# Values in two groups a visit, and one landing place for queries and keys, in a threshold attention with token and channel MLPs

## The chip, the cores and the metric

One NeuronCore of one Trainium2 chip runs the whole program. The metric is the device time of one execution in microseconds, here the median of the runs shown. Everything is float32 on the engines; TensorE runs each float32 matmul as two instructions.

The engines are named as in the profile: PE is TensorE's matrix multiply and PEld its loading of weights, DVE is VectorE, ACT is ScalarE, POOL is GpSimd, and SP is SyncE, which computes nothing here and issues transfers. SPq and ACTq are the queues on which SP and ACT issue transfers.

## The reference

Inputs are q, k and v of shape (8 batches, 8 heads, 576 tokens, 64), a threshold `tau` of 0.02, and four weight matrices, which arrive as 64-bit floats.

```
scores = (q @ k^T) / 8
keep the scores within tau of their row's maximum, set the rest to -1e9
attn = softmax(scores);  x = attn @ v, heads laid side by side: (8, 576, 512)
u = x + (relu(x^T @ w_tok1) @ w_tok2)^T        # over tokens, 576 -> 256 -> 576
out = u + relu(u @ w_ch1) @ w_ch2              # over channels, 512 -> 1536 -> 512
```

## The kernel before

Heads are worked in pairs, four pairs to a batch, 32 pairs in all. Two pairs (a half batch) are cut into 9 units: units 0 to 3 are the 128-row blocks of the first pair, unit 4 is shared and holds the last 64 rows of both pairs, and units 5 to 8 are the 128-row blocks of the second pair. The program has 144 units, 18 to a batch, in one hand-written loop over `u` (L534 to L587); every engine takes its instructions in the order in which that loop writes them, and so do the transfer queues.

For each unit the loop writes, in this order:

- `scores(u)` (L287): 8 TensorE instructions (16 in the shared unit) into the PSUM tiles `sc`, one for each head; DVE takes the row maxima (L306), POOL turns them into biases (L307).
- `norm(u-1)` (L327): DVE's reciprocal of the row sums, POOL's scaling of the previous unit's exponentials `e` (L334).
- The transposition of unit u-2. In batch 0 TensorE does it through PSUM (`turn`, L345). From batch 1 on (`in_blocks`) DVE transposes 32x32 blocks into a tile `T` (L368) and SP's queue moves the blocks into place with 16 transfers (L378) into a tile `eT`, once a group is complete. A group is two units of one pair (rows 0 to 255, or 256 to 511), or the shared unit alone.
- A share of the MLP steps that the previous batch left (`fill`), then `weigh(u)` (L310): ACT's two Prelus (L316), a share of `fill`, two exponentials (L323) with a share of `fill` behind each. A batch's MLP steps are queued by `push` when its last values group is written, and `fill` spreads them by their estimated costs over the next batch's units.
- The loads of queries and keys of a later pair (`load_qk`, L97), in quarters of 32 partitions, q and k each: 8 transfers of 72 KB for a pair; in batch 0 SP issues them, later ACT. `load_v` issues one transfer of a pair's values.
- `prep` (L278): DVE transposes a pair's loaded queries and keys into `qT` and `kT` (L283), which have two places each. It is written in units 2 and 7 of a half batch.
- The values groups that are due (`values`, L390): 20 TensorE instructions, L408 and L413, in pairs that use half of the array's columns each, into a PSUM tile `pv` (`pv_s` for the shared rows), and ACT's copy of it into `xT` (L418). PSUM has two tiles (`ps_tr`) for this, shared with the transposes.

In batch 0 the loop also converts the weights from 64 bits to float32 in 31 pieces (`weight`, `load_piece`): SP loads a piece (L176) into one of four raw places, ACT takes two steps (L191, L193), DVE three (L201, L205, L209), POOL one (L215). The conversion goes on in batch 1, whose units also carry batch 0's MLP. ACT, DVE, POOL and SP meet these steps in the same queues as the units' own work.

A group's values are written two units after its transposition (one in batch 0). Within the 9 units of a half batch, counted from its first, the groups from batch 1 on come at the end of unit 5 (first pair, rows 0 to 255), 7 (first pair, rows 256 to 511), 8 (shared, two small groups), 1 of the next half (second pair, first rows) and 3 of the next half (second pair, last rows).

Of the kernel before, what the change touches and what calls it, by code (L numbers as in the profile page):

```python
# [9 lines left out]
F32 = mybir.dt.float32  # L10
# [7 lines left out]
P = 128  # L18
# [3 lines left out]
def kernel(  # L22
# [26 lines left out]
    nc = tc.nc  # L49
    B, H, S, D = q.shape  # L50
# [14 lines left out]
    NK = 2 * S // P  # L65
# [4 lines left out]
    ld = ctx.enter_context(tc.tile_pool(name="ld", bufs=2))  # L70
    work = ctx.enter_context(tc.tile_pool(name="work", bufs=2))
# [11 lines left out]
    pairs = [(b, p) for b in range(B) for p in range(NP)]  # L83
# [9 lines left out]
    loaded = {}  # L93
    VL = 4
    vlast = [const.tile([P, P], F32, name=f"vl{i}") for i in range(VL)]

    def load_qk(n, eng, part=None):  # L97


        b, p = pairs[n]  # L100
        if n not in loaded:
            loaded[n] = [ld.tile([P, S // 32, 32], F32, tag=tag, name=f"{tag}_{n}") for tag in ("lq", "lk")]
        for i in range(4) if part is None else (part,):
            h, c = divmod(i, 2)
            for src, t, on in zip((q, k), loaded[n], eng):
                on.dma_start(
                    out=t[32 * i : 32 * i + 32], in_=src[b, 2 * p + h, :, 32 * c : 32 * c + 32].rearrange("(n t) d -> t n d", t=32)
                )

    def load_v(n):  # L110

        b, p = pairs[n]
        lv = ld.tile([P, NK, D], F32, tag="lv", bufs=4, name=f"lv_{n}")
        nc.sync.dma_start(out=lv, in_=v[b].rearrange("h s d -> (h s) d")[2 * S * p : 2 * S * p + 2 * S, :].rearrange("(c p) d -> p c d", p=P))
        vals[n] = lv
# [51 lines left out]
    def load_piece(i):  # L167
        if i >= len(pieces):
            return
        dst, src = pieces[i]  # L170
        rows = dst.shape[0]
        n = 1
        for d in dst.shape[1:]:
            n *= d
        raw = raw_at[i % NRAW][0:rows, 0 : n * (2 if wide(i) else 1)].bitcast(src.dtype)
        nc.sync.dma_start(out=like(raw, dst), in_=src)  # L176
        if wide(i):
            words = raw.bitcast(U32).rearrange("p (n w) -> p n w", w=2)
            h2 = work.tile([P, WMAX], F32, tag="o", name=f"h2_{i}")[0:rows, 0:n]
            raws[i] = like(words[:, :, 0], dst), like(words[:, :, 1], dst), like(h2, dst)  # L180
        else:
            raws[i] = like(raw, dst)
# [40 lines left out]
    def weight(n):  # L223

        nonlocal steps_done
        for k in range(steps_done, min(steps_done + n, 3 * len(pieces) + 1)):
            i, part = divmod(k, 3)
            if part == 0:
                on_gpsimd(i - 1)
                if i:  # L230
                    load_piece(i - 1 + NRAW)
            else:
                on_scalar(i + 1, part - 1)
            on_vector(i, part)
            steps_done = k + 1
# [3 lines left out]
        weight(3 * i + 4 - steps_done)  # L239

    load_piece(0)
    load_qk(1, (nc.sync, nc.sync))
    load_v(0)
    for i in range(1, NRAW):
        load_piece(i)
# [26 lines left out]
    eTs = {}  # L272
    Ts = {}

    def in_blocks(b):
        return b > 0

    def prep(n):  # L278
        lq, lk = loaded.pop(n)
        made = []  # L280
        for src, name in ((lq, "qT"), (lk, "kT")):
            sb = work.tile([P, S], F32, tag=name, name=f"{name}_{n}")
            nc.vector.transpose(out=sb, in_=src.rearrange("p n d -> p (n d)"))  # L283
            made.append(sb)
        heads[n] = made
# [41 lines left out]
    def norm(u):  # L327
        e, rs = st[u]
        rr = small.tile([P, 2], F32, tag="rr", name=f"rr_{u}")
        nc.vector.tensor_scalar(out=rr, in0=rs, scalar1=1e-9, scalar2=None, op0=ALU.add)  # L330
        nc.vector.reciprocal(out=rr, in_=rr)  # L331
        for h in range(2):
            eh = e[:, S * h : S * h + S]
            nc.gpsimd.tensor_scalar(out=eh, in0=eh, scalar1=rr[:, h : h + 1], scalar2=1.0, op0=ALU.mult, op1=ALU.mult)  # L334
        st[u] = e

    def group_of(u):

        b, p0, t = units[u]
        if t == SHARED:  # L340
            return (b, p0, "s"), 0, 1
        i, c = divmod(t - (t > SHARED), NI)
        return (b, p0 + i, c // 2), c % 2, 2

    def turn(u, third):  # L345

        key, place, n = group_of(u)
        e = st[u]
        if third == 0 and place == 0:
            eTs[key] = work.tile([P, NK * 2 * P], F32, tag="eT", name=f"eT_{u}")  # L350
        if third == 2:
            st.pop(u)
        eT = eTs[key][:, 0 : NK * n * P].rearrange("p (c x) -> p c x", c=NK)
        ps = ps_tr.tile([P, MAIN], F32, tag="tr", name=f"tr{third}_{u}")[:, 0 : 3 * P].rearrange("p (c x) -> p c x", c=3)
        for c in range(3):
            k0 = (3 * third + c) * P
            nc.tensor.transpose(out=ps[:, c, :], in_=e[:, k0 : k0 + P], identity=ident)
        on = nc.scalar.copy if third == 1 and u % 2 else nc.vector.tensor_copy
        on(out=eT[:, 3 * third : 3 * third + 3, P * place : P * place + P], in_=ps)

    def turn_blocks(u):

        key, place, n = group_of(u)
        e = st.pop(u)
        if place == 0:
            Ts[key] = work.tile([P, NK * 2 * P], F32, tag="T", name=f"T_{u}")
        T = Ts[key][:, 0 : NK * n * P]
        nc.vector.transpose(  # L368
            out=T.rearrange("p (a c n x) -> p c a n x", a=4, c=NK, n=n)[:, :, :, place, :],
            in_=e.rearrange("p (c a x) -> p c a x", c=NK, a=4),  # L370
        )
        if place == n - 1:
            del Ts[key]
            eTs[key] = work.tile([P, NK * 2 * P], F32, tag="eT", name=f"eT_{u}")
            w = NK * n * 32
            for a in range(4):
                for i in range(4):
                    nc.sync.dma_start(  # L378
                        out=eTs[key][32 * a : 32 * a + 32, w * i : w * i + w], in_=T[32 * i : 32 * i + 32, w * a : w * a + w]
                    )  # L380

    def split_middle(n):

        lv, vl = vals[n], vlast[n % VL]
        for h in range(2):
            r = slice(D * h, D * h + D)
            nc.gpsimd.tensor_copy(out=vl[r, r], in_=lv[r, NI, :])
        vals[n] = lv, vl
# [140 lines left out]

    prep(0)  # L530
    due = deque()
    b_now = 0
    LAG = 2
    for u in range(len(units) + LAG + 4):  # L534
        on = u < len(units)
        if u == UB:
            late.close()
            ps_mm = ctx.enter_context(tc.tile_pool(name="ps_mm", bufs=2, space=bass.MemoryType.PSUM))
        if on:
            b_now, p0, t = units[u]  # L540
            n = b_now * NP + p0
        w = u - LAG
        back = 0 <= w < len(units)
        if on:
            scores(u)
        if 0 < u <= len(units):
            norm(u - 1)
        if b_now:
            weight(2)
        if back:  # L550
            key, place, many = group_of(w)
            if in_blocks(key[0]):
                turn_blocks(w)
            else:
                for i in range(3):
                    turn(w, i)
            if place == many - 1:
                b, p, c = key
                if c == 0 and p % 2 == 0:
                    split_middle(b * NP + p)  # L560
                if c == "s":
                    split_middle(b * NP + p + 1)
                when = u + (2 if in_blocks(b) else 1)
                due += [(when, b, p + i, c) for i in range(2 if c == "s" else 1)]
        if b_now:
            fill(0.4)
        weight(2 if b_now else 1)
        if on:
            weigh(u)
        elif b_now:  # L570
            fill(0.6)
        weight(2 if b_now else 1)
        if on:
            m = n + 2 + t // 4
            if t < 8 and m < len(pairs):
                load_qk(m, (nc.scalar if b_now else nc.sync,) * 2, t % 4)
                if t % 4 == 3:
                    load_v(m)
            if t == 2:
                prep(n + 1)  # L580
            if t == 7 and n + 2 < len(pairs):
                prep(n + 2)
        while due and due[0][0] <= u:
            _, b, p, c = due.popleft()
            values(b, p, c)
            if p == NP - 1 and c == 1:
                push(b)  # L587
# [31 lines left out]
```

## Time and profile before

| | |
|---|---|
| median of 3 runs | 1392.27 us (1392.06 to 1392.32) |
| profiled execution | 1392.27 us, span 1390.5 us |
| TensorE, matmuls | 1325.5 us busy, 95% of the span |
| DVE | 586.8 us, 42% |
| ACT | 590.0 us, 42% |
| POOL | 357.8 us, 26% |
| granted TensorE clock, mean | 0.991 |
| matmuls: channel MLP, first (L468) / second (L484) | 398.6 / 389.1 us |
| matmuls: scores (L301) | 190.1 us |
| matmuls: values, 128x256 groups (L408 / L413) | 42.4 / 123.5 us |

The span runs from the first to the last instruction. The 40 slices of a page are 34.8 us each; a digit is the busy share in tenths. Rows of a timeline give the start, the length, the engine, the line, the operation with output and inputs, and how many instructions of that kind follow each other; the bracket at the end is the engine's idle time ahead of the row and what ended it. A row of the chain of waits gives a start, a length and what the time went to. TensorE's instructions are pipelined, so rows that follow each other overlap a little; starts are what to subtract.

### The profile page before, as it was taken

What the parts mean: (1) busy time and instruction counts of PE and PEld (TensorE: products, weight loads), DVE (VectorE), ACT (ScalarE), POOL (GpSimd) and SP (SyncE); (2) the same over time, 40 slices, a digit from 0 to 9 for tenths busy, and PEclk for the clock granted to TensorE, in tenths of its full rate; (3) what the DMA queues carried; (4) which work ended last, traced back from release to release, by engine and by line L of the source; (5) the groups of instructions that cost most, each with busy time, mean ns of one, the idle gap of its engine ahead of it and who ended that gap; (6) DMA issues with size and microseconds to landing.
All of it is one profiled execution on the core that took longest, in us unless ns stands there. A gap on an engine that the chain in (4) does not pass through costs nothing.

```text
span 1390.5 us, 19515 instructions
## 1 busy us (share of the span) xinstructions
PE 1325.5 (95%) x6866; PEld 831.8 (60%) x6866; DVE 586.8 (42%) x1009; ACT 590.0 (42%) x1328; POOL 357.8 (26%) x683
## 2 busy tenths in 40 slices
PE   6776899999999999999999999999999999999998
PEld 3443475646565566665766567465657566575675
DVE  6788784444444444434244344433343453101000
ACT  5776564444454444443434435353434444120110
POOL 4566563232222222212122222221221222000000
PEclk9998899999999999999999999999999999999999
DMA  6444654444444434433433444443433433300000
GB/s 132 97 115 125 185 140 122 109 120 93 107 118 107 105 86 97 109 84 79 110 85 92 104 96 102 98 105 79 99 91 89 103 76 85 84 8 16 8 8 23
DMA packets 257376, 128.34 MB, mean 92 GB/s; under 512 B 208064, under 2 KB 221376, under 8 KB 257280
## 3 DMA queue, kind: packets, MB, share of 16 engines
q1 hardware_dynamic: 131632, 111.46, 30.5%
q10 hardware_dynamic: 125648, 15.64, 7.1%
q8 instruction: 55, 0.90, 0.3%
q14 instruction: 41, 0.34, 0.1%
HBM read 43.25 MB, written 9.44 MB: 38 GB/s over the span
## 4 chain that ended last, share of the span: by engine, by line
PE 86%; DVE 6%; DMA 2%; ACT 2%; SPq 2%; POOL 1%; issue 1%; DVEq 0%; ACTq 0%
PE c L484 27%; PE c L468 26%; PE sc L301 11%; PE pv L413 7%; PE t L439 5%; PE t L446 3%; PE pv L408 2%; DVE mx L306 2%; PE tx L430 1%; SPq L378 1%; PE c L480 1%; PE pv_s L413 1%; DVE T L368 1%; DMA scratch<-in_moe_w_ch_dram 1%; ACT e L316 1%
## 5 line engine op out<-in xcount | busy, mean ns | idle before, releaser
L306 DVE TENSOR_REDUCE mx<-sc 128x1 f32<-128x576 f32 x288 | 204.7, 751 | 523.1 <-PE sc L301 521.1
L468 PE MATMUL c<-xT,wc 128*128 128x256 f32 (+1 forms) x1920 | 398.6, 361 | 0.5 <-ACT g L469 0.4
L484 PE MATMUL c<-wc,g 128*128 128x512 f32 x864 | 389.1, 596 | 0.0
L468 PEld LDWEIGHTS c<-xT,wc 128*128 128x128 f32 x1920 | 334.3, 190 | 69.7 <-issue 27.6
L307 POOL TENSOR_SCALAR bias<-mx,toff 128x1 f32<-128x1 f32 x288 | 79.6, 277 | 814.9 <-DVE mx L306 757.9
L316 ACT ACTIVATE e<-sc,bias 128x576 f32<-128x576 f32 x288 | 199.2, 739 | 155.5 <-POOL bias L307 155.1
L484 PEld LDWEIGHTS c<-wc,g 128*128 128x128 f32 x864 | 157.9, 190 | 175.3 <-issue 173.2
L469 ACT ACTIVATE g<-c 128x256 f32<-128x256 f32 (+1 forms) x240 | 86.7, 361 | 335.5 <-PE c L468 330.6
L334 POOL TENSOR_SCALAR e<-e,rr 128x576 f32<-128x576 f32 x288 | 218.8, 772 | 16.0 <-DVE rr L331 3.8
L323 ACT ACTIVATE e<-e,ntau 128x576 f32<-128x576 f32 x288 | 220.6, 771 | 0.0
L301 PE MATMUL sc<-kT,qT 64*128 64x288 f32 (+1 forms) x1280 | 190.1, 435 | 14.2 <-DVE kT L283 7.2
L368 DVE STREAM_TRANSPOSE T<-e 128x1152 f32<-128x1152 f32 x126 | 172.5, 1369 | 16.3 <-DMA eT<-T 9.6
L301 PEld LDWEIGHTS sc<-kT,qT 64*128 64x128 f32 (+1 forms) x1280 | 103.7, 179 | 90.0 <-issue 47.6
L413 PE MATMUL pv<-eT,lv 128*64 128x256 f32 x1024 | 123.5, 384 | 0.0
L413 PEld LDWEIGHTS pv<-eT,lv 128*64 128x64 f32 x1024 | 75.1, 139 | 37.5 <-issue 0.8
L489 DVE COPY o<-c 128x512 f32<-128x512 f32 x36 | 24.5, 679 | 160.8 <-PE c L484 160.8
L446 PE MATMUL t<-w,a 128*128 128x288 f32 x256 | 79.0, 438 | 13.6 <-DVE xT L450 10.4
L418 ACT COPY xT<-pv 128x256 f32<-128x256 f32 x64 | 23.8, 372 | 160.0 <-PE pv L413 147.2
L439 PE MATMUL t<-x_sb,w 128*128 128x512 f32 x160 | 73.2, 605 | 0.7 <-ACT g L469 0.7
L446 PEld LDWEIGHTS t<-w,a 128*128 128x128 f32 x256 | 46.8, 198 | 41.4 <-DVE xT L450 18.4
L450 DVE TENSOR_TENSOR xT<-xT,t 128x288 f32<-128x288 f32 x64 | 28.0, 441 | 81.9 <-PE t L446 81.9
L323 ACT ACTIVATION_READ_ACCUMULATOR e<-e,ntau 128x1 f32 x288 | 56.5, 196 | 0.0
(48 smaller groups left out, 603.2 us busy)
## 6 DMA issues: line engine op xcount, KB each, us to landing
eT<-T SPq DMA_DIRECT2D x896, 72.0 KB, 2.1
scratch<-in_moe_w_ch_dram SPq DMA_DIRECT2D x24, 512.0 KB, 4.0
lv<-in_v_dram SPq DMA_DIRECT2D x32, 288.0 KB, 3.3
out_dram<-o SPq DMA_DIRECT2D x36, 256.0 KB, 2.2
eT<-T SPq DMA_DIRECT2D x224, 36.0 KB, 1.9
lk<-in_k_dram ACTq DMA_DIRECT2D x108, 72.0 KB, 2.8
lq<-in_q_dram ACTq DMA_DIRECT2D x104, 72.0 KB, 2.1
lq<-in_q_dram SPq DMA_DIRECT2D x24, 72.0 KB, 3.4
```

The costliest lines, as they stand in the source:

```text
L301: nc.tensor.matmul(sc[h][rows, f, 0:HS], lhsT=qT[r, cols], rhs=kT[r, HS * f : HS * f + HS], start=True, stop=True)
L306: nc.vector.tensor_reduce(out=mx[:, c], in_=sc[h][:, :, 0:HS], axis=AX.XY, op=ALU.max)
L316: nc.scalar.activation(out=eh, in_=sc[h][:, :, 0:HS], func=AF.Prelu, bias=bias[:, h : h + 1], scale=SCALE, alpha=STEEP)
L323: nc.scalar.activation(out=eh, in_=eh, func=AF.Exp, bias=ntau, accum_out=rs[:, h : h + 1])
L334: nc.gpsimd.tensor_scalar(out=eh, in0=eh, scalar1=rr[:, h : h + 1], scalar2=1.0, op0=ALU.mult, op1=ALU.mult)
L368: nc.vector.transpose(out=T.rearrange("p (a c n x) -> p c a n x", a=4, c=NK, n=n)[:, :, :, place, :], in_=e.rearrange("p (c a x) -> p c a ...
L413: nc.tensor.matmul(to[r], lhsT=lv[:, j, :], rhs=eT[:, j], start=False, stop=(c == NI - 1), skip_group_check=True)
L439: nc.tensor.matmul(ps, lhsT=w1[:, t, P * m : P * m + P], rhs=x_sb[:, t, :], start=(t == 0), stop=(t == NT - 1))
L446: nc.tensor.matmul(ps, lhsT=s["a"][:, m, P * c : P * c + P], rhs=w2[:, m, HS * f : HS * f + HS], start=(m == 0), stop=(m == NTK - 1))
L468: nc.tensor.matmul(ps, lhsT=wc1[:, j, c, :], rhs=uT[:, c, GR * i : GR * i + n], start=(c == 0), stop=(c == NCC - 1))
L469: nc.scalar.activation(out=s["g"][:, j, 0:n], in_=ps, func=AF.Relu)
L484: nc.tensor.matmul(flat, lhsT=s["g"][:, j, P * t : P * t + P], rhs=wc2[:, j, :], start=False, stop=(j == NJ - 1), skip_group_check=True)
```

## The change

Three things change.

1. From batch 1 on, a complete values group is held back until another can go with it. In a half batch the first pair's two groups are now written one behind the other at the end of unit 7; the shared unit's two small groups and the second pair's first group at the end of unit 1 of the next half; the second pair's last group alone at the end of unit 3, as before.
2. The shared unit's transposed exponentials get a tile of their own, half the size (`eT1`, one place); `eT` keeps two places.
3. The loaded queries and keys (`lq`, `lk`) have one place each instead of two. A pair's 8 transfers are spread so that they are issued between the transposes of the pair before and their own: for a half batch's first pair two each in units 3, 4, 5 and 6 of the half batch before it (transposes in unit 7), for its second pair three in unit 8 before it, three in unit 0 and two in unit 1 (transposes in unit 2). The loads for pair 1, which were issued ahead of the first weight pieces, are now issued in units 0 and 1.

`weigh`, `scores`, `norm`, the MLP steps and the weight conversion are the same in both.

```diff
-    def load_qk(n, eng, part=None):
+    def load_qk(n, eng, parts=range(8)):
         b, p = pairs[n]
         if n not in loaded:
-            loaded[n] = [ld.tile([P, S // 32, 32], F32, tag=tag, name=f"{tag}_{n}") for tag in ("lq", "lk")]
-        for i in range(4) if part is None else (part,):
+            loaded[n] = [ld.tile([P, S // 32, 32], F32, tag=tag, bufs=1, name=f"{tag}_{n}") for tag in ("lq", "lk")]
+        for part in parts:
+            i, which = divmod(part, 2)
             h, c = divmod(i, 2)
-            for src, t, on in zip((q, k), loaded[n], eng):
-                on.dma_start(
-                    out=t[32 * i : 32 * i + 32], in_=src[b, 2 * p + h, :, 32 * c : 32 * c + 32].rearrange("(n t) d -> t n d", t=32)
-                )
+            eng[which].dma_start(
+                out=loaded[n][which][32 * i : 32 * i + 32],
+                in_=(q, k)[which][b, 2 * p + h, :, 32 * c : 32 * c + 32].rearrange("(n t) d -> t n d", t=32),
+            )
...
     load_piece(0)
-    load_qk(1, (nc.sync, nc.sync))
     load_v(0)
...
+    def eT_tile(u, n):
+        tag, bufs = ("eT1", 1) if n == 1 else ("eT", 2)
+        return work.tile([P, NK * n * P], F32, tag=tag, bufs=bufs, name=f"{tag}_{u}")
...
-            eTs[key] = work.tile([P, NK * 2 * P], F32, tag="eT", name=f"eT_{u}")
+            eTs[key] = eT_tile(u, n)
...
-                when = u + (2 if in_blocks(b) else 1)
-                due += [(when, b, p + i, c) for i in range(2 if c == "s" else 1)]
+                group = [(b, p + i, c) for i in range(2 if c == "s" else 1)]
+                if in_blocks(b):
+                    held += group
+                    if (p % 2, c) in ((0, 1), (1, 0), (1, 1)):
+                        due += [(u + 2,) + g for g in held]
+                        held.clear()
+                else:
+                    due += [(u + 1,) + g for g in group]
...
-            m = n + 2 + t // 4
-            if t < 8 and m < len(pairs):
-                load_qk(m, (nc.scalar if b_now else nc.sync,) * 2, t % 4)
-                if t % 4 == 3:
-                    load_v(m)
+            when = {3: (2, 0, 2), 4: (2, 2, 4), 5: (2, 4, 6), 6: (2, 6, 8), 8: (3, 0, 3), 0: (1, 3, 6), 1: (1, 6, 8)}
+            if u == 0:
+                load_qk(1, (nc.sync, nc.sync), range(0, 3))
+            if t in when:
+                m, lo, hi = when[t]
+                if n + m < len(pairs):
+                    load_qk(n + m, (nc.scalar if b_now else nc.sync,) * 2, range(lo, hi))
+            if t in (3, 7) and n + 2 + t // 4 < len(pairs):
+                load_v(n + 2 + t // 4)
```

More of the change, by code (lines that the diff above doesn't have):

```diff
@@ L373, in turn_blocks @@
             del Ts[key]
-            eTs[key] = work.tile([P, NK * 2 * P], F32, tag="eT", name=f"eT_{u}")
+            eTs[key] = eT_tile(u, n)
             w = NK * n * 32
@@ L531 @@
     due = deque()
+    held = []
     b_now = 0
```

## The prediction

> **What bounds the kernel now.** I read the busy shares first, then the 40 slices, then TensorE's instructions in order of time through a middle stretch, then the start and the passage from batch 0 to batch 1, where TensorE is not full.
>
> ```profile
> PE 1325.5 (95%) x6866; PEld 831.8 (60%) x6866; DVE 586.8 (42%) x1009; ACT 590.0 (42%) x1328; POOL 357.8 (26%) x683
> ...
> PE   6776899999999999999999999999999999999998
> ...
> PEclk9998899999999999999999999999999999999999
> ```
>
> TensorE is full from the sixth slice (174 us) to the end; before that it is 60 to 80% busy and other things set the pace. So a saving behind 174 us must be TensorE's own time, and one ahead of it must shorten a chain of waits. The timeline of TensorE in batch 1:
>
> ```profile
> 401.80 1.24 PE L301 MATMUL sc<-kT,qT 64*128 64x288 f32 x8
> 402.97 5.45 PE L468 MATMUL c<-xT,wc 128*128 128x256 f32 x24
> 408.34 0.65 PE L408 MATMUL pv<-eT,vl 128*64 128x256 f32 x4
> 408.83 1.90 PE L413 MATMUL pv<-eT,lv 128*64 128x256 f32 x16
> 410.65 1.24 PE L301 MATMUL sc<-kT,qT 64*128 64x288 f32 x8
> 411.82 5.45 PE L468 MATMUL c<-xT,wc 128*128 128x256 f32 x24
> 417.20 1.24 PE L301 MATMUL sc<-kT,qT 64*128 64x288 f32 x8
> ...
> 468.79 0.34 PE L408 MATMUL pv_s<-eT,vl 128*64 128x64 f32 x4
> ...
> 469.42 0.29 PE L408 MATMUL pv_s<-eT,vl 128*64 128x64 f32 x4
> ...
> 470.11 1.24 PE L301 MATMUL sc<-kT,qT 64*128 64x288 f32 x8
> ```
>
> Units start at each "sc". With a values group the unit takes 8.85 us (401.80 to 410.65), with the same 24 matmuls and no values 6.55 (410.65 to 417.20): a values visit costs 2.30 us. It is 10 pairs of concurrent 256-column instructions; 8 single ones of that width take 1.73 us in the chain at 169.94, 0.216 each, so the arithmetic is 2.16 us and changing over costs at most 0.15. Of the shared unit's two small groups the first takes 0.63 (468.79 to 469.42) and the second, followed by scores, 0.69: leaving the values form costs about 0.05.
>
> The start, from the chain of waits:
>
> ```profile
> 9.72 0.50 SPq L114
> 10.26 5.31 DMA scratch<-in_moe_w_tok_dram
> 15.60 0.69 ACT scratch L191
> 16.28 0.55 ACT h L193
> 16.83 0.63 ACT e L316
> 17.50 2.30 PE sc L301 x4
> ```
>
> The second weight piece is issued at 10.26 because eight loads of the next queries and keys go ahead of it on SP's queue (4.41 to 9.68). ScalarE stands idle 1.94 us for it, and unit 1's Prelus queue behind.
>
> **The change part by part.**
>
> *Start.* The eight loads leave SP's queue ahead of the pieces. The second piece is then issued near 4.9 us (0.40 of piece 0 and 0.50 of the values' load after 3.73) and, at 5.31 us, lands near 10.2, ahead of ScalarE's being free at 13.65. The wait of 1.94 goes; next late is the Prelu's own bias, at 14.97, so units 1 and 2 move up by about 1.9. Ends: 0, if a fixed beat further on takes it back, and -3.5, if the first values group (3.47 us of L413 at 32.61; the granted clock was 0.50 from 32.8 to 36.2) falls in a full-clock stretch as well (1.90 at 44.35). I take **-1.9**: the chain from there to 70 us is DVE, PE and ACT in turn, with little idle to swallow it.
>
> *One place for queries and keys.* No instruction is added: 16 loads for each pair of head pairs, as before, at 2, 2, 2, 2, 3, 3, 2 in a unit, and the transposes stay where they were. But a pair's last two loads now come one unit ahead of its transposes, in batch 0 on SP right behind a 512 KB piece. There the trace has 3.5 to 3.7 us from issue to landing:
>
> ```profile
> 67.54 0.51 SPq L106 DMA_DIRECT2D lq<-in_q_dram  x1
> ...
> 70.67 0.76 DVE L283 STREAM_TRANSPOSE qT<-lq 128x576 f32<-128x576 f32 x1
> ```
>
> Loads at 46.70, 67.54 and 93.92 with 3.6, 3.5 and 3.5 us land at 50.30, 71.04 and 97.42; DVE wants them at 50.64, 70.67 and 97.24. So waits of 0, 0.37 and 0.18: **+0.55**, and since DVE is 80 to 90% busy there and scores follow at once, it counts in full. Behind the waiting transposes are the maxima of the next unit, then POOL's bias and the Prelus. Ends: 0, and 3 x 2.5 = 7.5, if every one lands like the slowest load of the run (6.0 us). From batch 1 on ScalarE issues them, and a unit of 6.5 us or more lies between; in batch 1 the loads at 446.24 are followed by transposes at 456.29: nothing. That a load must wait for the place to be free costs nothing either: the transposes that free it stand on DVE ahead of the maxima that the issuing unit's Prelus need.
>
> The Trainium skill's entry page (Trainium Kernel Development and Optimization, Best Practices) says to double-buffer so that transfers overlap compute, which speaks against one place. The row above is the answer here: the transposed copies keep their two places, and the load still has a unit's time. By the rule alone each of 31 later loads would lie open, an estimate of 31 x 3.5 = 108 us.
>
> *Into batch 1.* The first held group leaves its unit at 157.23, where TensorE is not the bound, for one that ends at 180, where it is:
>
> ```profile
> 157.23 1.12 PE L408 MATMUL pv<-eT,vl 128*64 128x256 f32 x4
> 158.14 2.38 PE L413 MATMUL pv<-eT,lv 128*64 128x256 f32 x16
> 160.46 1.24 PE L301 MATMUL sc<-kT,qT 64*128 64x288 f32 x8
> ```
>
> Gone is 3.23 us (the granted clock was 0.50 from 152.4 to 159.0) ahead of these scores, whose maxima DVE awaits, idle 2.53 us until 161.73. DVE's own work ends at 159.19, so 2.5 is what it can move up. Later the group costs 2.30. Net **-0.2**; ends -0.9 (all 3.23 gained) and +2.3 (none).
>
> *Two groups a visit.* For 7 batches x 2 halves, two visits are merged away. Where two full groups join, at most 0.15 and at least 0.05 goes, I take 0.10; where the two small groups join the next full one, 0.05, the small groups' own row. 14 x 0.10 + 14 x 0.05 = **-2.1**; ends -2.8 and -1.4. Units that lose their visit get as short as 4.77 us (434.26, less 2.30). Scores need the previous Prelus: a unit of 4.34 (285.73) had its next scores at the usual 1.17, one of 3.21 (470.11) stretched them to 1.83. So nothing is lost there. The shared unit's own half-size tile and the longer hold take no instruction; DMAs on SP keep their order.
>
> The Trainium skill, TensorEngine Tiling (Array Packing), Key Properties, says a change of tiling mode drains the array. The rows above bound that drain at 0.15; with the 166 ns constant of TensorE: Matmul & The Clock Gate (Single matmul latency) for each merge, an estimate, it would be 28 x 0.166 = 4.6 us.
>
> *A third tile in one visit.* There are two PSUM tiles for these groups, so the full group behind two small ones must wait until ScalarE has copied the first. That copy starts 0.85 after its group (469.64 against 468.79), takes 0.21, and a release takes some 0.05: 1.11, ahead of the 1.26 that the two groups last. But ScalarE must be free: in the visits of these 14 units it was busy (exponentials, then two load issues) until 1.89, 1.00, 1.00, 1.13, 1.20 and 1.25 us after the first values matmul in six of them, at most 0.39 in the rest. Wait = that time - 1.00: 0.89 + 0.13 + 0.20 + 0.25 = **+1.5**. Ends 0 and 14 x 0.89 = 12.5; I keep near the six rows since they are the same units with the same ScalarE work. Queued behind on TensorE is the next unit's scores.
>
> *Sum*: -1.9 + 0.55 - 0.2 - 2.1 + 1.5 = -2.15. The profiled execution took 1392.27 us (span 1390.5 and 1.8 around it), which is the median of the three runs as well. So **1390.1 us**.
>
> **The rivals.**
>
> A: every gain comes and ScalarE is never late for the first small group. For it: eight of 14 visits have it free. -1.9 + 0 - 0.9 - 2.8 + 0 = -5.6, **1386.7**. Against: load issues fall in just those units.
>
> B: the merging does not do what it says (a group boundary inside a visit costs as much as a change of form) and only the start and the late copies count: -1.9 + 0.55 - 0.2 + 1.5 = -0.05, **1392.2**.
>
> C, slower: the single place makes DVE wait in batch 0. Place: L283's transposes of head pairs 2, 3 and 4. Price: 7.5 us in place of 0.55, so **1397.1**. For it: half a microsecond of slack or less in all three, and a piece of 512 KB right ahead in the same queue. Against: the three measured stretches all gave 3.3 to 3.7. It decides (over 0.2% slower) from 5.5 us of wait together.
>
> **How the numbers follow.** Forecast 0.50, with 1387.5 to 1393 as its own range, in which nearly half lies below 1389.5; A 0.18; B 0.12; C 0.20. Below 0.2% (2.8 us), about what a measurement can tell here, it counts as the same. Faster: 0.18 + 0.22 = 0.40; same: 0.28 + 0.12 = 0.40; slower: C, 0.20. The range runs from A's 1386.5 to C's 1397, leaving out about a tenth at either end: the first because half-clock stretches ahead of 180 us (granted clock 0.83 in 120 to 160 us) may shift by a group's 0.9 to 1.6 us either way, the second for landing times and the third tile's upper end.
>
> **What would show it.** Right: ScalarE's wait ahead of the second L191 gone; DVE's L283 waiting for lq or lk under 1 us in all; two full groups back to back taking 4.4 to 4.5 us; TensorE waiting for ScalarE's xT copies ahead of a values group by about 1.5 us in all. Wrong: DVE waiting several microseconds for lq or lk before 100 us (C); no idle ahead of the third group (A); a merged visit of 4.6 us (B); or the scores of batch 1's seventh unit no earlier than now against their Prelus, which would turn the passage into a loss of 2.3.

## The result, and the profile after

| | before | after |
|---|---|---|
| median of the runs side by side | 1392.3 us (1391.84 to 1394.64) | 1399.8 us (1396.66 to 1404.05) |
| after / before, 95% interval | | 1.0053 (1.0034 to 1.0073) |
| profiled execution | 1392.27 us, span 1390.5 | 1398.72 us, span 1396.9 |

The change made the kernel slower by 7.4 us (4.7 to 10.2); the forecast was 1390.1. The page of the kernel after, busy shares and two of the rows of 40 slices:

```profile
PE 1325.2 (95%) x6866; PEld 834.5 (60%) x6866; DVE 587.4 (42%) x1009; ACT 591.0 (42%) x1328; POOL 358.7 (26%) x683
...
PE   6777789999999999999999999999999999999998
...
PEclk9998899999999999999999999999999999999999
```

No engine has noticeably more to do: TensorE was busy 1325.5 and is busy 1325.2 us, VectorE 586.8 and 587.4, ScalarE 590.0 and 591.0. The 6.4 us of span are waits, and where TensorE is full a wait lengthens the run by its whole length (in unit 100, below, 1.34 us of wait in place of 0.37 make 0.97). The waits of TensorE's second token matmuls, in the kernel before, and of these and its values, after (engine and line, what it waited for, total us, times, longest). Before, no values matmul waits for ScalarE's copies in this view:

```profile
PE t L446 <- DVE xT L450: 10.4, 8, 2.6
PE t L446 <- ACT g L469: 3.1, 6, 0.8
```

```profile
PE t L450 <- DVE xT L454: 14.9, 11, 3.4
PE pv L412 <- ACT xT L422: 4.7, 4, 3.5
...
PE t L450 <- ACT g L473: 2.4, 4, 0.8
```

Two things are new: values wait for ScalarE's copies (4.7 us in four large waits, and some smaller ones that this view counts with the weight loads), and the second token matmul waits more often for VectorE's addition. Only the first was in the prediction. (L412, L417, L422, L450, L454 and L472 are what L408, L413, L418, L446, L450 and L468 were before.)

**The third tile.** TensorE's timeline in the first visit that holds two small groups and a full one:

```profile
199.26 0.34 PE L412 MATMUL pv_s<-eT,vl 128*64 128x64 f32 x4
...
199.89 0.29 PE L412 MATMUL pv_s<-eT,vl 128*64 128x64 f32 x4
...
204.18 0.65 PE L412 MATMUL pv<-eT,vl 128*64 128x256 f32 x4 [3.54 <-ACT xT L422]
```

ScalarE's timeline over the same stretch (ACTq rows are issues of transfers):

```profile
201.34 0.20 ACT L323 ACTIVATION_READ_ACCUMULATOR e<-e,ntau 128x1 f32 x1
201.99 0.34 ACTq L106 DMA_DIRECT2D lq<-in_q_dram  x1
203.25 0.35 ACTq L106 DMA_DIRECT2D lk<-in_k_dram  x1
203.92 0.33 ACT L422 COPY xT<-pv_s 128x64 f32<-128x64 f32 x2 [2.38 <-DMA lq<-in_q_dram]
```

The copy that frees the PSUM tile could have run from about 200.1 (0.85 us behind its group, as in the kernel before). ScalarE finishes its exponentials at 201.54, then issues two loads 1.26 us apart, and copies at 203.92; TensorE stands for 3.54 us. The chain of waits shows what the first load's issue waited for:

```profile
199.99 1.98 DMA eT<-T
...
201.99 1.93 DMA lq<-in_q_dram
203.92 0.22 ACT xT L422
...
204.18 0.65 PE pv L412 x4
```

The issue at 201.99 comes 0.02 us behind the landing (201.97) of a transfer of transposed exponentials that SP had issued at 199.99. The second, at 203.25, comes 0.02 us behind the landing (203.23) of another of these, issued at 201.18. In the trace each load has the same semaphore as the transfer ahead of it, and the issue waits for that semaphore. In the next three visits the second load follows such a landing by 0.02 us as well (271.65, 344.16, 413.10). In the same unit of the kernel before the two issues run during the exponentials, 0.40 us apart (199.84 and 200.24), more than 1.5 us behind the last landing on their semaphores. Why the program shares the semaphores in this way these runs do not show. The full group should start 1.21 us behind the first small one, as it does where nothing waits. In the 14 visits it started 4.92, 1.62, 1.79, 1.92, 1.21, 1.22, 1.22, 1.48, 1.36, 1.21, 1.22, 1.52, 1.36 and 1.22 us behind: 6.3 us of waits in all, 3.7 of them in this one visit and 1.7 in the next three.

**The joint.** TensorE's timeline of two full groups that are written one behind the other, after:

```profile
863.44 0.65 PE L412 MATMUL pv<-eT,vl 128*64 128x256 f32 x4
...
865.64 0.60 PE L412 MATMUL pv<-eT,vl 128*64 128x256 f32 x4
...
867.90 1.24 PE L301 MATMUL sc<-kT,qT 64*128 64x288 f32 x8
```

From 863.44 to 867.90 are 4.46 us, where two separate visits took 2 x 2.30 = 4.60. A joint saves about 0.15 us. (The other sort of joint, two small groups and a full one, is shown in the first experiment.)

**The single place.** VectorE's transposes of head pair 3 (L283), after:

```profile
70.82 0.78 DVE L283 STREAM_TRANSPOSE qT<-lq 128x576 f32<-128x576 f32 x1 [0.55 <-DMA lq<-in_q_dram]
```

Those of pairs 2 and 4 (50.17 and 97.37) wait for nothing.

### The profile page after: what moved, and what is told of

The parts are those of the page before. It is cut to its first block, busy times and chain, and to the rows that moved or that the text cites. A ratio compares the mean times of both kernels' runs of the same rounds, so it can differ in the third digit from the quotient of the medians.

```text
span 1396.9 us, 19563 instructions
## 1 busy us (share of the span) xinstructions
PE 1325.2 (95%) x6866; PEld 834.5 (60%) x6866; DVE 587.4 (42%) x1009; ACT 591.0 (42%) x1328; POOL 358.7 (26%) x683
## 4 chain that ended last, share of the span: by engine, by line
PE 84%; DVE 7%; DMA 3%; SPq 2%; ACT 2%; issue 1%; POOL 1%; ACTq 0%; DVEq 0%; POOLq 0%
PE c L488 26%; PE c L472 25%; PE sc L301 11%; PE pv L417 7%; PE t L443 5%; PE t L450 3%; DVE mx L306 3%; SPq L382 2%; PE pv L412 2%; DVE T L372 1%; PE tx L434 1%; DMA eT<-T 1%; PE c L484 1%; ACT e L316 1%; ACT e L323 1%
## 5 line engine op out<-in xcount | busy, mean ns | idle before, releaser
L472 PE MATMUL c<-xT,wc 128*128 128x256 f32 (+1 forms) x1920 | 398.7, 361 | 1.1 <-DVE xT L454 0.5
L472 PEld LDWEIGHTS c<-xT,wc 128*128 128x128 f32 x1920 | 334.4, 190 | 70.4 <-issue 27.2
L417 PE MATMUL pv<-eT,lv 128*64 128x256 f32 x1024 | 125.1, 387 | 0.0
L417 PEld LDWEIGHTS pv<-eT,lv 128*64 128x64 f32 x1024 | 75.9, 141 | 39.2 <-issue 4.0
L450 PE MATMUL t<-w,a 128*128 128x288 f32 x256 | 79.9, 443 | 17.3 <-DVE xT L454 14.9
L422 ACT COPY xT<-pv 128x256 f32<-128x256 f32 x64 | 23.7, 372 | 131.0 <-PE pv L417 123.2
L450 PEld LDWEIGHTS t<-w,a 128*128 128x128 f32 x256 | 47.9, 202 | 45.3 <-DVE xT L454 22.7
L454 DVE TENSOR_TENSOR xT<-xT,t 128x288 f32<-128x288 f32 x64 | 28.0, 441 | 84.8 <-PE t L450 84.8
```

The lines of the kernel that those rows point to most:

```text
L417: nc.tensor.matmul(to[r], lhsT=lv[:, j, :], rhs=eT[:, j], start=False, stop=(c == NI - 1), skip_group_check=True)
L450: nc.tensor.matmul(ps, lhsT=s["a"][:, m, P * c : P * c + P], rhs=w2[:, m, HS * f : HS * f + HS], start=(m == 0), stop=(m == NTK - 1))
L472: nc.tensor.matmul(ps, lhsT=wc1[:, j, c, :], rhs=uT[:, c, GR * i : GR * i + n], start=(c == 0), stop=(c == NCC - 1))
```

## The experiments

Each kernel ran beside the kernel before on the same chip, which took 1393.5 or 1393.6 us there, so what is compared is the ratio to it; "x us" behind a ratio is its distance from 1 times 1392.3. After itself stands at 1.0053, from 6 executions; its interval is wide, so a difference "below after" is known to about 3 us either way.

### One PSUM tile for the two small groups

```diff
+        if pair and p % 2 == 0:
+            small_ps[b] = ps_tr.tile([P, MAIN], F32, tag="tr", name=f"pv_{b}_{p}_{c}")
+        if pair:
+            both = small_ps[b][:, 0 : 2 * N].rearrange("p (i x) -> p i x", i=2)
+            ps = both[:, p % 2, :]
...
+        if pair:
+            if p % 2:
+                at = S * (b % 2) + tok
+                nc.scalar.copy(out=xTs[b][:, p - 1 : p + 1, at : at + N], in_=both)
+            return
```

> The changed kernel, but the shared unit's two small values groups (from batch 1 on) go into two parts of one PSUM tile and are copied by one ACT instruction, so that the full group behind them has the second tile to itself. Theory 1 (the full group waits for ACT's copy of the first small group: 6.3 us in the trace of the changed kernel, third group at up to 4.92 us after the first instead of 1.21): these waits go, all 14 visits put the full group at 1.2 us, time 1399.8 - 6.3 = 1393.5 us. Rival (the later loads of queries and keys and the held group that moved into the full stretch are what costs): no change beyond 1 us, 1399.

Measured: 1393.46 us, 0.9999 (0.9987 to 1.0011). TensorE's timeline of the same visit in this kernel, whose values are L420 and L425:

```profile
200.27 0.34 PE L420 MATMUL pv_s<-eT,vl 128*64 128x64 f32 x4
...
200.90 0.29 PE L420 MATMUL pv_s<-eT,vl 128*64 128x64 f32 x4
...
201.48 0.60 PE L420 MATMUL pv<-eT,vl 128*64 128x256 f32 x4
...
203.74 1.24 PE L302 MATMUL sc<-kT,qT 64*128 64x288 f32 x8
```

The full group starts 1.21 us behind the first small one here, and 1.21 or 1.22 in all 14 visits, though ScalarE's copy comes at 203.99, behind the same two loads. The wait for the third tile is gone and with it 7.5 us (1.0053 - 0.9999), against 6.3 read from the trace. The visit takes 3.47 us (200.27 to 203.74); apart, the small groups take 0.63 + 0.69 and the full one 2.30, 3.62 together. So this joint saves 0.15 us too.

### Queries and keys issued behind the values

```diff
-            if t in when:
-                m, lo, hi = when[t]
-                if n + m < len(pairs):
-                    load_qk(n + m, (nc.scalar if b_now else nc.sync,) * 2, range(lo, hi))
...
             values(b, p, c)
             if p == NP - 1 and c == 1:
                 push(b)
+        if on:
+            if t in when:
+                m, lo, hi = when[t]
+                if n + m < len(pairs):
+                    load_qk(n + m, (nc.scalar if b_now else nc.sync,) * 2, range(lo, hi))
```

> The changed kernel, but each unit's loads of queries and keys are written behind its values groups instead of ahead of them, so that ACT's copies do not queue behind load issues. Theory 1a (the copy is late because of the two loads ahead of it on ACT's queue, in six of the eight visits that wait): the waits that remain are those behind ACT's own computing, about 1.5 us in the first visit and 0.3 in one other, so 4.5 us of 6.3 go: 1395.3 us. Rival (ACT's exponentials are what makes the copy late): 6.3 stays, 1399.8.

Measured: 1393.66 us, 1.0003 (0.9994 to 1.0013), 7.0 us below after. ScalarE's timeline in the same visit: the copy now runs as soon as the exponentials are done, and the loads follow.

```profile
201.72 0.21 ACT L323 ACTIVATION_READ_ACCUMULATOR e<-e,ntau 128x1 f32 x1
201.82 0.33 ACT L422 COPY xT<-pv_s 128x64 f32<-128x64 f32 x2
...
204.52 0.35 ACTq L106 DMA_DIRECT2D lq<-in_q_dram  x1
205.18 0.37 ACTq L106 DMA_DIRECT2D lk<-in_k_dram  x1
```

The same loads, the same three groups and two tiles, only the order on ScalarE's queue: so it is the load issues ahead of the copy that made it late. By the trace 0.9 us of the 6.3 remain, 0.75 of them in this visit, behind ScalarE's exponentials, so 5.4 went, near the 4.5 expected; the 7.0 of the runs agrees with both within the interval.

### The full group ahead of the two small ones

```diff
-                    held += group
+                    held[:] = group + held if (p % 2, c) == (1, 0) else held + group
```

> The changed kernel, with the full group ahead of the two small ones in the second visit of each half batch; PSUM tiles and loads as in the change. The copy that the third group waits for is now that of the full group; it stands behind the same loads on ScalarE, but TensorE does 2.3 + 0.65 us of work before it needs the tile, where it did 1.21 us. Theory (the third tile's wait is set by the copy behind the loads): the 6.3 us of waits shrink to the units whose copy came more than 2.9 us late, about 1.6 us, 1399.8 - 4.7 = 1395.1 us. Rival (the wait is set by the loads' share of TensorE's or the values' own path, whatever the order): no change, 1399.8 us.

Measured: 1394.78 us, 1.0012 (1.0003 to 1.0021), 5.7 us below after. One large wait is left, in the first such visit (the third group, now a small one, at 206.77, 4.22 us behind the first; 1.26 us of idle). As expected: what counts is how much TensorE has to do before it needs the tile back.

### The shared groups not held

```diff
-                    if (p % 2, c) in ((0, 1), (1, 0), (1, 1)):
+                    if (p % 2, c) != (0, 0):
```

> The changed kernel, but the shared unit's small groups are not held: only the first pair's two full groups are joined. Theory 1 with its second part (the units 8 and 0, shorter by the small groups' 1.31 us, let the token MLP's matmuls of unit 1 run into DVE's additions, 2.8 us in three units): both go, and so does the saving of 0.15 in each of 14 joints, 2.1: 1399.8 - 6.3 - 2.8 + 2.1 = 1392.8 us. If only the PSUM tiles mattered, 1395.6. Rival (loads and passage): 1399 or more.

Measured: 1394.59 us, 1.0010 (1.0000 to 1.0019). No visit has three groups, and the wait is gone here too, but so are half of the joints. It is 1.4 us slower than before, where 0.5 was expected. The second part of the expectation fails: the small groups are back in their own units, and the second token matmuls still wait 15.0 us for VectorE in 11 waits (10.4 in 8 before). So it was not the shorter units that made these waits.

### Nothing held

```diff
-                    if (p % 2, c) in ((0, 1), (1, 0), (1, 1)):
+                    if True:
```

> The changed kernel with no group held: the values are where they were, and what is left of the change is the single place for queries and keys, the later loads and the shared unit's own tile. By the comparison of the two traces unit by unit the start gains 0.5, the transposes of pair 3 lose 0.4 and nothing else differs: 1392.2 us, the same as the kernel before. Rival (the loads cost): 1395 to 1399.

Measured: 1397.01 us, 1.0031 (1.0020 to 1.0041). A miss, and the most useful one: without any holding the change still costs 4.3 us. The loads, the half-size tile and the start, which were to win 1.35 us together, lose. Against the kernel above, 14 joints of two full groups are worth 2.9 us here (14 x 0.15 = 2.1 by the trace). What the 4.3 us are is taken apart in the runs that follow: 2.8 come from tiles, the rest was not found.

Unit by unit the trace of this kernel is later than before in units 64, 83, 100 and 136, by 0.81, 0.35, 0.96 and 0.97 us, each time because a second token matmul waits for VectorE's addition. No group is held there. TensorE's timeline of unit 100 in the kernel before, then in this one:

```profile
804.85 1.24 PE L446 MATMUL t<-w,a 128*128 128x288 f32 x4 [0.37 <-ACT g L469]
```

```profile
806.84 1.24 PE L450 MATMUL t<-w,a 128*128 128x288 f32 x4 [1.34 <-DVE xT L454]
```

The same matmul waits for ScalarE's Relu in one and for VectorE's addition in the other. Both are readers of a PSUM tile of the pool of two that all MLP results share, so the matmul has been given the other tile. The order of the 356 MLP results is the same in both programs, but 183 of them sit in the other tile: 91 from the exchange in unit 64 to that in unit 100, and all from unit 136 to the end (the 181 in the next expectation is a miscount). The four kernels above have it as well.

### The MLPs' tiles as before

In this kernel and the next three, each result's tile is written out by hand instead of being left to the pool; `MM` is a number of 356 bits, one for each result in order.

```diff
+    def mm_tile(shape, dtype, tag, name):
+        at = 355 - mm_count[0]
+        mm_count[0] += 1
+        return ps_mm.tile(shape, dtype, tag=tag + str((MM >> at) & 1), name=name)
...
-            ps = ps_mm.tile([P, HS], F32, tag="mm", name=f"t2_{b}_{c}_{f}")
+            ps = mm_tile([P, HS], F32, tag="mm", name=f"t2_{b}_{c}_{f}")
...
-            ps_mm = ctx.enter_context(tc.tile_pool(name="ps_mm", bufs=2, space=bass.MemoryType.PSUM))
+            ps_mm = ctx.enter_context(tc.tile_pool(name="ps_mm", bufs=1, space=bass.MemoryType.PSUM))
```

> The changed kernel, with one thing put back: each of the 356 results of the two MLPs gets the PSUM tile (of the two in the pool mm) that it had in the kernel before. In the changed program 181 of the 356 sit in the other tile, and at three places (units 64, 100 and 136) a token-MLP matmul therefore waits for VectorE's addition where it waited for ScalarE's Relu before. Theory (the tiles were dealt out anew): the 0.8 + 1.0 + 1.0 = 2.8 us of units 64, 100 and 136 go, 1399.8 - 2.8 = 1397.0 us. Rival (ScalarE's extra load issues themselves make the MLPs late, whichever tile they use): no change, 1399.8 us.

Measured: 1397.5 us, 1.0025 (1.0014 to 1.0036), 3.9 us below after. Its trace has the kernel before's waits for ScalarE's Relu again (3.1 us, 6 times), and units 64, 100 and 136 are each 0.8 us shorter than after.

### The kernel before with the new tiles

The same edit to the kernel before, with `MM` from the changed program:

```diff
-            ps = ps_mm.tile([P, HS], F32, tag="mm", name=f"t2_{b}_{c}_{f}")
+            ps = mm_tile([P, HS], F32, tag="mm", name=f"t2_{b}_{c}_{f}")
```

> The kernel before, with only the PSUM tiles of the two MLPs dealt out as in the changed kernel: no load, no value and no exponential is touched. Theory (the tiles were dealt out anew): 0.8 + 1.0 + 1.0 us of new waits of the token-MLP matmuls for VectorE's addition, 1392.3 + 2.8 = 1395.1 us. Rival (ScalarE's load issues): no change, 1392.3 us.

Measured: 1396.24 us, 1.0015 (1.0004 to 1.0026): 2.1 us slower (0.6 to 3.6). TensorE's timeline of unit 100 in this kernel, where t is L454:

```profile
806.85 1.24 PE L454 MATMUL t<-w,a 128*128 128x288 f32 x4 [1.34 <-DVE xT L458]
```

The wait is there to 0.01 us, with the loads of the kernel before. Units 64, 100 and 136 are 0.82, 0.97 and 0.97 us longer, 2.76 together. Unit 83 isn't, so its 0.35 has another cause. That the tiles cost this is shown; why the building of the program dealt them out otherwise is not. What differs near those units is where the loads are issued (three in the unit ahead of each, where the kernel before has two), but no run tried that by itself.

### Nothing held, the MLPs' tiles as before

```diff
-                    if (p % 2, c) in ((0, 1), (1, 0), (1, 1)):
+                    if True:
...
-            ps = ps_mm.tile([P, HS], F32, tag="mm", name=f"t2_{b}_{c}_{f}")
+            ps = mm_tile([P, HS], F32, tag="mm", name=f"t2_{b}_{c}_{f}")
```

> The kernel without any held values (its time was 1397.0 us), with the PSUM tiles of the two MLPs as before. Theory (the tiles were dealt out anew): 1397.0 - 2.8 = 1394.2 us, and what is left above 1392.3 lies in the start and batch 0. Rival (ScalarE's load issues): 1397.0 us.

Measured: 1394.53 us, 1.0012 (1.0003 to 1.0022), 2.6 us below the kernel without the tiles mended. From unit 27 on its trace now lags the kernel before by a steady 0.95, and by 1.27 behind unit 83. So the 1.7 us that remain (0.4 to 3.1) lie, but for unit 83, in batch 0 and the first units of batch 1. The 13th unit starts 1.4 us earlier than before. Then 0.45 are lost where the transposes of pair 3 wait 0.63 us for their load, and 1.93 in the unit behind, where TensorE's granted clock is 0.50 from 74.6 to 81.4 us (1.00 there in the kernel before). Unit 26 waits for a weight piece that lands later (ScalarE idle 4.36 us for it, 3.39 before), and the stretches at half clock between 100 and 160 us fall otherwise. That stretch at half clock near 74 us is in four of the ten traces with one place for queries and keys and in none of the four with two; whether the loads bring it about isn't shown. No single cause of these was tried apart.

### The start alone

```diff
-    load_qk(1, (nc.sync, nc.sync))
...
+            if u == 0:
+                load_qk(1, (nc.sync, nc.sync))
             m = n + 2 + t // 4
```

> The kernel before, with only the start changed: the second pair's queries and keys are no longer asked for between the first and the second weight piece, but behind the first unit. Both places for queries and keys, all values and the MLPs' PSUM tiles stay. By the prediction's start term: 1392.3 - 1.9 = 1390.4 us. By the trace of the changed kernel (first scores 1.60 us later because the first keys land later, 2.07 us won back at the second piece): 1392.3 - 0.5 = 1391.8 us.

Measured: 1392.3 us, 0.9995 (0.9985 to 1.0006): between 2.1 us faster and 0.8 slower. In its trace the first scores start at 7.14 us (7.16 before) and the fourth unit's at 20.14 (22.20 before): 2.06 us won, near the 1.9 of the prediction, and its last scores start 1.96 earlier. The runs neither confirm nor exclude that much. That the keys land later because the pieces go first, as this expectation said of the changed kernel, isn't borne out: here the pieces go first too, and the keys are not late. The MLPs' tiles are dealt as before here: units 64, 100 and 136 take what they took.

### All the mends

One tile for the small groups, loads behind the values, the MLPs' tiles as before, and no value held in batch 1:

```diff
-                    if (p % 2, c) in ((0, 1), (1, 0), (1, 1)):
+                    if b == 1 or (p % 2, c) in ((0, 1), (1, 0), (1, 1)):
```

> The changed kernel with all the mends together: both small groups of a shared unit in one PSUM tile with one copy, the query and key loads of a unit written behind its values, the MLPs' PSUM tiles as before, and no value held in batch 1, so that the joined visits begin with batch 2. Theory: 1399.8 - 6.3 (wait for the third tile) - 2.8 (MLP tiles) - 1.1 (passage into batch 1) = 1389.6 us, below the kernel before. Rival (the tiles don't matter): 1392.4 us.

Measured: 1391.3 us, 0.9982 (0.9973 to 0.9991): 2.5 us faster than before (1.3 to 3.8), 9.9 faster than after.

The same with values held from batch 1 on:

```diff
-                    if b == 1 or (p % 2, c) in ((0, 1), (1, 0), (1, 1)):
+                    if (p % 2, c) in ((0, 1), (1, 0), (1, 1)):
```

> The kernel with all the mends (2.5 us under the kernel before), but with the values held from batch 1 on, as in the change. By the prediction's term for the passage into batch 1 (a gain of 0.2 us): 1392.3 - 2.7 = 1389.6 us. By the trace of the changed kernel (0.82 us won in units 23 and 24, 2.16 us paid later in batch 1): 1392.3 - 2.5 + 1.1 = 1390.9 us.

Measured: 1390.76 us, 0.9982 (0.9974 to 0.9991). Between the two there is no difference, to within 1.7 us. So the passage into batch 1 is worth nothing that shows; the loss of 1.1 us that I read from one trace of after isn't confirmed.

### Joined values alone

The kernel with all the mends and no value held in batch 1, with `load_qk`, its two places and its times of the kernel before; the pool `small` gives up a buffer to make room.

```diff
-    small = ctx.enter_context(tc.tile_pool(name="small", bufs=6))
+    small = ctx.enter_context(tc.tile_pool(name="small", bufs=5))
...
+    load_qk(1, (nc.sync, nc.sync))
     load_v(0)
...
+            m = n + 2 + t // 4
+            if t < 8 and m < len(pairs):
+                load_qk(m, (nc.scalar if b_now else nc.sync,) * 2, t % 4)
+                if t % 4 == 3:
+                    load_v(m)
```

> Joined values alone: two places for queries and keys and the loads as in the kernel before, both small groups in one PSUM tile, values held from batch 2 on, the MLPs' PSUM tiles as before (the pool of small tiles is cut from 6 to 5 buffers to make room). Theory: 13 visits x 2 joints x 0.15 us = 3.9 us off and nothing lost in the start, batch 0 and batch 1, 1392.3 - 3.9 = 1388.4 us. Rival (the new loads cost nothing once the tiles are mended): the same as the kernel with all the mends, 1392.3 - 2.5 = 1389.8 us.

Measured: 1390.35 us, 0.9974 (0.9965 to 0.9982): 3.6 us faster than before, the fastest of all. The waits of the second token matmul are those of the kernel before again, to the digit:

```profile
PE t L471 <- DVE xT L475: 10.4, 8, 2.6
PE t L471 <- ACT g L494: 3.1, 6, 0.8
```

The trace has 12 visits of each sort, so 24 joints (not the 26 of the expectation); at 0.15 us they are 3.6, which is what was measured. The gap of 1.1 us to the kernel with the new loads lies within both intervals: that the new loads still cost something there is likely, but not shown.

## Why the prediction was wrong

The forecast was 2.15 us faster; it is 7.4 slower, above the range (1386.5 to 1397.0; rival A's own sum gives 1386.7). By the terms of its sum:

| term | predicted | trace | runs |
|---|---|---|---|
| start | -1.9 | -2.06 with the first scores at the same time | -0.7 (-2.1 to +0.8) alone |
| late queries and keys | +0.55 | +0.55 in pair 3, 0 in pairs 2 and 4 | +1.7 (0.4 to 3.1) with the start, nothing held, tiles as before |
| passage into batch 1 | -0.2 | not to be told from the clock | 0, to within 1.7 |
| joints | -2.1 | 28 x 0.15 = -4.2 | -3.6 for 24 |
| third tile | +1.5 | +6.3 | +7.5, +7.0 (mended in two ways, each to within about 3) |
| MLPs' PSUM tiles | not in it | +2.8 (nothing held), +2.4 (after) | +3.9, +2.1, +2.6 |

**Third tile: the mechanism was right, the size was the step that failed.** The step was "the same units with the same ScalarE work". ScalarE's end of work was read from the units as they were before, where both issues ran during the exponentials, and "1.89 us behind the first values matmul" became more than 4 in the first visit. That an issue can itself have to wait was not allowed for: after, the second issue waits for the landing of a transfer of SP's in each of the four visits that lose 5.4 of the 6.3 us. The upper end of 12.5 held it, but I stayed near the six rows, and the value that I took went into the forecast.

**"From batch 1 on ... nothing" is the second step that failed.** The moved loads were costed by when they land. But the pool's tiles were dealt out anew in the built program, and three matmuls outside the change wait for another engine. None of the rivals had it. Rival C, the slower one, put the loss at VectorE's transposes in batch 0; their waits were what the forecast said.

**Joints: right in kind, too small.** I took 0.10 and 0.05 for the two sorts and bounded them by 0.15; both sorts save 0.15. The small groups' own row (0.05) counts only what leaving the values form costs, and not what entering it does. The Trainium skill's constant of 166 ns (TensorE: Matmul & The Clock Gate, Single matmul latency), taken for each merge, was nearer: an estimate of 4.6 us, against 4.2 in the trace. The page gives it for a single matmul and not for a change of form, so that it comes near may be chance.

**Start and single place: right by their waits, wrong in their sum.** The wait for the second piece went, and the units moved up by 2.06. The profiled execution of after doesn't show it in the end, since its first scores came 1.60 us later (8.76 against 7.16), which is scatter, as the last section shows. The Trainium skill's rule on double-buffering (Trainium Kernel Development and Optimization, Best Practices), taken alone, would have made the loads lie open; the trace has 0.55 us of it, in one pair of 32. But with nothing held and the tiles as before, start, single place and later loads together made the kernel 1.7 us slower (0.4 to 3.1), where the two terms gave -1.35. This is the third step that failed, that nothing else in batch 0 would move; where its 3 us come from stays open.

Together: -2.06 + 0.55 - 4.2 + 6.3 + 2.8 = +3.4 us by the trace's terms. The late first scores add 1.6, which makes 5.0 of the 6.4 us between the two profiled spans. The rest is spread over batch 0 and the first units of batch 1 and was not taken apart. With the measured +1.7 in place of the first two terms the sum is +1.7 - 4.2 + 6.3 + 2.8 = +6.6, against 7.4 (4.7 to 10.2). The same terms give 1.7 - 4.2 + 6.3 = +3.8 with the MLPs' tiles as before (+3.5 measured) and 1.7 - 4.2 = -2.5 with all the mends and values held from batch 1 on (-2.5 measured).

## What to carry to other kernels

When a copy out of PSUM sits on the queue that also issues loads, ask of every issue ahead of it what it waits for itself, and order the queue so that what TensorE waits for comes first: reordering alone won 7.0 of the 7.4 us lost here (within about 3). After any edit, compare the built programs' waits outside the edit too; a pool that deals out tiles by itself can exchange two of them hundreds of instructions away, and the wait that this makes looks as if it belonged to the change. Then try the parts alone, since the part with the gain (the joints) was hidden beneath two losses that could each be mended, and a third that wasn't found.

## What the runs showed of the hardware that was not expected

- Two load issues on ScalarE's queue held its next instruction for 2.38 us (201.54 to 203.92), where the issues themselves are 0.34 and 0.35 us long: each came 0.02 us behind the landing of a transfer that SP had issued (201.97 and 203.23). In the kernel before, the same unit's two issues are 0.40 us apart (199.84 and 200.24) and run while ScalarE computes.
- The first keys land at different times in different runs, whatever is queued behind them: the first scores start at 7.14 to 9.71 us over the traces. Of the kernels with the old order of loads one has 7.16, one 7.27 and one 9.71; with the new order 7.14 to 9.52. A single profiled start is therefore uncertain by more than the term that the prediction made of it.
- A stay in one matmul form is worth 0.15 us for each change of form and back that it saves, the same for 64-column and 256-column groups (4.46 us against 2 x 2.30, and 3.47 against 3.62).
